# Routed attention and gated MLP on one core: f32 weights cast by GpSimd's DMAs instead of by the engines, in a new written order

## The chip, the cores and the metric

The kernel runs on one core of one Trainium2 chip. The metric is the device time of one execution, in microseconds (us). The engines are TensorE (PE in the profile, with its weight loads as PEld), VectorE (DVE), ScalarE (ACT), GpSimd (POOL) and SyncE (SP), which here only issues DMAs.

## The reference

Attention over 4 batches and 8 heads, 768 positions, head dimension 64. Each query and key is assigned to the nearest of 16 centroids of its head, and a query sees only keys of its own cluster. An MLP with a SiLU gate follows.

```python
q_assign = argmax(normalized(q) @ normalized(centroids).T)      # per head; the same for k
scores = where(q_assign[:, None] == k_assign[None, :], q @ k.T / 8, -1e9)
attn = softmax(scores) @ v                                      # [4, 8, 768, 64]
x = attn.transpose(0, 2, 1, 3).reshape(3072, 512)
h = x @ w_in                                                    # w_in [512, 2048], f32
out = (h * sigmoid(h)) @ w_out                                  # w_out [2048, 512], f32
```

## The kernel before, in words

All matmuls are in f16. Work is cut into steps: `step(engs, cost, fn, after, use, key)` notes a step with the engines that may run it (`"POOL/DVE/ACT"`), the steps it follows and the buffers it uses. Nothing is issued then. `Plan.emit` issues the steps in the sequence of a table, `ORDER`, with the engine that `CHOICE` names for each (the first one where it names none) and the buffer that `PLACES` gives. Negative entries of `ORDER` are filler matmuls on zeros: -1602 is 16 of them. So the order on each engine is written out by hand of a planner that is not part of the kernel; each engine works its own list strictly in that order, and so does each DMA queue. All loads but two, all stores and all DMA transposes are on SP's queue.

The steps, per pair of heads `p` and batch `b`:

- `load`: q, k and v in f32 to a buffer of the pool `raw` (8 buffers of 4 KB per partition, shared by q, k, v and, before, the weights).
- `part`: each row is split in two f16 halves, `hl` ("hi", a scaled copy, L295 to L297 or L291 by engine; "lo", the remainder, L441 on DVE). `hl` is transposed to `ab`: for the first pieces on PE (L466) with a copy back from PSUM, for all others by a DMA transpose of SP (L454). PE multiplies `ab` with the centroids (`stk`, `nstk`; L492, L493, L495), DVE takes the sum (L512), the peak (L523), marks the winner (`oh`, L536) and transposes the marks in 32 x 32 blocks (`ohT`, L550). Four "puts" write the marks into rows 64 to 79 of `ab`, so that the scores matmul itself carries the mask. A put runs on DVE (L295), POOL (L297) or ACT (L291).
- `attention`: scores on PE (L595), exp on ACT to `P` (L602), the product with v on PE (L612). `cast_values` makes `vt`, the f16 values, from `raw`.
- `normalize` (L631, L648) divides by the sums, to `xn`; `turn_x` transposes it to `xt`.
- `mlp`: up-projection on PE (L701) with `win_s`, tanh on ACT (`tn`, L712), the gate on DVE (`gq`, L715), down-projection on PE (L730) with `wout_s`, a copy to `ot` and a store (L745).
- `weight`: brings in one of the sixteen pieces of the MLP weights, 256 rows of 512 numbers as a 128 x 2 x 512 tile, 512 KB of f32. SP loads it to a `raw` buffer (L763), then POOL, DVE or ACT casts it to `win_s` or `wout_s` (L293 on POOL and DVE). `w_in_done` and `w_out_done` hold the step that the matmuls wait for.

The MLP of a batch follows that batch's attention, and in the order it is interleaved with the attention of later batches, so that PE has work while ACT does exp. Before its first real work PE runs the filler matmuls (`warm`, L853).

Of the kernel before, what the change touches and what calls it, by code (L numbers as in the profile page):

```python
# [17 lines left out]
BLOCKS = [[0, 2], [2, 6]]  # L18
UNITS = [[0, 4], [4, 6]]

ORDER = [
# [181 lines left out]
def kernel(  # L203
# [10 lines left out]
    nc = tc.nc  # L214
# [471 lines left out]
    def mlp(b, j0, j1, key):  # L686
# [36 lines left out]
        for t in range(j1 - j0):  # L723
# [26 lines left out]
            step("SP", ("store", 2048, 128), store, after=[x], use=[ot], key=-500)  # L750


    def weight(kind, n, key, after=()):
        x = buf("raw")

        def f(e):
# [128 lines left out]
```

## Time and profile before

| | us |
|---|---|
| three runs | 318.61, 319.30, 315.93 (median 318.61) |
| the profiled execution | 315.72, span 313.9 |
| PE, DVE, ACT, POOL busy | 297.7, 212.6, 221.0, 96.5 |
| first scores on PE, last matmul's end | 16.39, 310.34 |
| weight loads issued, first to last | 15.5 to 55.1 |
| weight casts on POOL (11) and DVE (5) | 12.6 and 4.0 |

The span runs from the first to the last instruction of the profiled execution, whose own time is 1.8 us longer. Busy time of PE includes matmuls that run slower than they could: their ends are modelled from the pipeline, so two matmuls that follow each other at any pace look like a busy engine. The table of 40 slices shows PE full from about 160 us on, with DVE and ACT dense before and thinner after it, and DMA engines full up to about 165 us.

### The profile page before, as it was taken

The numbers are of one execution on the slowest core, as the hardware profiler recorded it, in microseconds if no ns is written. First come the engines' busy times: TensorE is split into PE (matmuls) and PEld (weight loads), VectorE is DVE, ScalarE is ACT, GpSimd is POOL, SyncE is SP. The second block draws the span as 40 slices with busy tenths as digits, with TensorE's granted clock in tenths as the row PEclk, the third lists the DMA queues.
The fourth block names the chain that finished last, engine by engine and source line by source line (L and its number), as shares of the span: only waits on it lengthen the run. The fifth ranks groups of instructions, "written<-read, shape, count | busy, mean of one in ns | idle before, by whom it ended". The sixth has DMA issues, their size and how long they took to land.

```text
span 313.9 us, 7524 instructions
## 1 busy us (share of the span) xinstructions
PE 297.7 (95%) x2993; PEld 184.7 (59%) x2993; DVE 212.6 (68%) x476; ACT 221.0 (70%) x306; POOL 96.5 (31%) x175
## 2 busy tenths in 40 slices
PE   7799999997899999899899999999999999999995
PEld 5678675555546656657676465555665744555552
DVE  6978999987899898899799576232463532175230
ACT  3577989987799998699889869957787213264212
POOL 4875662544646364447226101300000000000000
PEclk9999999999999999999999999999999999999999
DMA  7989998969899999989992920000013021010023
GB/s 215 322 250 249 273 293 185 366 156 169 201 251 303 271 241 173 209 179 227 209 232 73 185 61 2 34 35 33 2 25 94 2 58 67 35 59 8 2 82 122
DMA packets 72852, 46.73 MB, mean 149 GB/s; under 512 B 52336, under 2 KB 65648, under 8 KB 72816
## 3 DMA queue, kind: packets, MB, share of 16 engines
q1 hardware_dynamic: 72528, 46.15, 59.2%
q8 instruction: 23, 0.38, 0.5%
q10 hardware_dynamic: 288, 0.10, 0.1%
q14 instruction: 13, 0.11, 0.1%
HBM read 27.30 MB, written 6.29 MB: 107 GB/s over the span
## 4 chain that ended last, share of the span: by engine, by line
PE 68%; DVE 11%; DMA 8%; POOL 5%; issue 3%; ACT 2%; SPq 1%; POOLq 0%; ACTq 0%; DVEq 0%
PE psum L730 23%; PE psum L701 22%; PE psum L595 14%; PE psum L612 7%; DMA ab<-hl 4%; DVE hl L441 2%; DMA raw<-in_k_dram 2%; POOL hl L297 2%; POOL ab L297 2%; PE psum L495 2%; DMA raw<-in_q_dram 2%; DVE gq L715 2%; DVE ab L295 1%; SPq L335 1%; DVE hl L295 1%
## 5 line engine op out<-in xcount | busy, mean ns | idle before, releaser
L602 ACT ACTIVATE P<-psum 128x1024 f16<-128x1024 f32 (+1 forms) x160 | 144.3, 942 | 24.5 <-PE psum L595 23.1
L715 DVE SCALAR_TENSOR_TENSOR gq<-tn,psum 128x512 f16<-128x512 f32 x96 | 63.2, 681 | 59.0 <-ACT tn L712 54.8
L701 PE MATMUL psum<-xt,win_s 128*128 128x256 f16 (+1 forms) x512 | 94.5, 325 | 1.3 <-DVE gq L715 1.0
L730 PE MATMUL psum<-wout_s,gq 128*128 128x512 f16 x384 | 90.9, 379 | 0.5 <-DVE wout_s L293 0.5
L595 PE MATMUL psum<-ab 80*128 80x256 f16 (+1 forms) x384 | 86.1, 339 | 3.1 <-POOL ab L297 2.2
L712 ACT ACTIVATE tn<-psum 128x512 f32<-128x512 f32 x96 | 56.0, 602 | 42.1 <-PE psum L701 39.7
L701 PEld LDWEIGHTS <-win_s 128*128 128x128 f16 x512 | 48.1, 97 | 33.1 <-issue 1.5
L297 POOL TENSOR_SCALAR ab<-ohT 16x384 f16<-16x384 f16 (+2 forms) x84 | 45.8, 546 | 62.0 <-DVE ohT L550 37.8
L730 PEld LDWEIGHTS <-gq 128*128 128x128 f16 x384 | 36.8, 97 | 41.4 <-issue 1.2
L612 PEld LDWEIGHTS <-P 128*128 128x128 f16 x1152 | 45.6, 99 | 13.4 <-issue 2.3
L612 PE MATMUL psum<-vt,P 128*128 128x65 f16 x1152 | 48.6, 195 | 1.9 <-POOL vt L293 1.2
L595 PEld LDWEIGHTS <-ab 80*128 80x128 f16 x384 | 34.6, 101 | 23.8 <-POOL ab L297 3.2
L441 DVE SCALAR_TENSOR_TENSOR hl<-raw,hl 128x384 f16<-128x384 f32 (+4 forms) x62 | 37.6, 622 | 8.3 <-POOL hl L297 7.9
L297 POOL TENSOR_SCALAR hl<-raw 128x384 f16<-128x384 f32 (+4 forms) x40 | 24.2, 609 | 25.6 <-DMA ab<-hl 9.2
L550 DVE STREAM_TRANSPOSE ohT<-oh 128x384 f16<-128x384 f16 (+2 forms) x33 | 18.5, 562 | 1.6 <-DVE oh L536 0.5
L648 DVE TENSOR_TENSOR xn<-psum,rz 128x384 f16<-128x384 f32 (+1 forms) x36 | 18.2, 509 | 0.8
L289 ACT COPY ot<-psum 128x512 f32<-128x512 f32 x14 | 8.1, 589 | 13.9 <-PE psum L730 13.7
L512 DVE TENSOR_REDUCE L<-psum 128x192 f32<-128x384 f32 (+1 forms) x28 | 14.9, 532 | 3.1 <-PE psum L495 2.7
L495 PEld LDWEIGHTS <-ab 128*128 128x128 f16 x320 | 11.7, 97 | 7.5 <-issue 2.4
L536 DVE TENSOR_TENSOR oh<-L,mx 128x96 f16<-128x96 f32 (+1 forms) x52 | 15.4, 313 | 0.6
L293 POOL CAST vt<-raw 128x384 f16<-128x384 f32 x23 | 12.7, 564 | 9.3 <-DMA raw<-in_v_dram 8.7
L295 DVE TENSOR_SCALAR ab<-ohT 16x384 f16<-16x384 f16 (+2 forms) x33 | 12.4, 375 | 0.9
(57 smaller groups left out, 146.4 us busy)
## 6 DMA issues: line engine op xcount, KB each, us to landing
raw<-in_v_dram SPq DMA_DIRECT2D x16, 384.0 KB, 4.8
out_dram<-ot SPq DMA_DIRECT2D x24, 256.0 KB, 2.3
raw<-in_k_dram SPq DMA_DIRECT2D x15, 384.0 KB, 5.5
raw<-in_q_dram SPq DMA_DIRECT2D x12, 384.0 KB, 4.6
raw<-in_moe_w_in_dram SPq DMA_DIRECT2D x8, 512.0 KB, 5.1
raw<-in_moe_w_out_dram SPq DMA_DIRECT2D x8, 512.0 KB, 5.6
raw<-in_q_dram SPq DMA_DIRECT2D x4, 256.0 KB, 5.2
ab<-hl SPq DMA_TRANSPOSE x28, 4.1
```

The source lines that it names most:

```text
L295: nc.vector.tensor_scalar(out=dst, in0=src, scalar1=scale, scalar2=None, op0=ALU.mult)
L297: nc.gpsimd.tensor_scalar(out=dst, in0=src, scalar1=scale, scalar2=1.0, op0=ALU.mult, op1=ALU.mult)
L441: (nc.vector if e == "DVE" else nc.gpsimd).scalar_tensor_tensor(out=dl, in0=src, scalar=scale, in1=dh, op0=ALU.mult, op1=ALU.subtract)
L550: nc.vector.transpose(t_(ohT)[:, 0:n, :].rearrange("p n c -> p (n c)"), t_(oh)[:, 0:n, :].rearrange("p n c -> p (n c)"))
L595: nc.tensor.matmul(o[:, w * (i - i0) : w * (i - i0 + 1)], t_(A)[0:80, kt[i], :], rhs, start=True, stop=True)
L602: nc.scalar.activation(out=t_(P)[:, 0:n], in_=o[:, 0:n], func=AF.Exp, bias=0.0, scale=-ESC)
L612: nc.tensor.matmul(bank(O)[:, D1 * (o0 + t) : D1 * (o0 + t + 1)], t_(P)[:, w * i + 128 * t : w * i + 128 * (t + 1)], t_(vb)[:, VW * j : VW ...
L648: nc.vector.tensor_tensor(out=x, in0=o, in1=z, op=ALU.mult)
L701: nc.tensor.matmul(bank(y)[:, n * (fb - f0) : n * (fb - f0 + 1)], win_s[:, r, ts(fb, 128)], t_(X)[:, r, 128 * j0 : 128 * j1], start=(r == ...
L712: nc.scalar.activation(out=t_(tn)[:, 0 : G * n], in_=bank(y)[:, 0 : G * n], func=AF.Tanh, bias=0.0, scale=1.0)
L715: nc.vector.scalar_tensor_tensor(out=t_(g)[:, f0 % 4 : f0 % 4 + G, 0:n], in0=t_(tn)[:, 0 : G * n].rearrange("p (g n) -> p g n", n=n), scal ...
L730: nc.tensor.matmul(bank(y), t_(gqs[quarter])[:, fc % 4, ts(t, 128)], wout_s[:, fc, :], start=(fc == 0), stop=(fc == NFB - 1),)
```

## The change

`SOFT = ['in', 'out']` names both weights. For these `weight` has one step instead of two: a DMA issued from GpSimd's queue that reads f32 from HBM and writes f16 straight to `win_s` or `wout_s`. No `raw` buffer and no cast belongs to it any more. The step waits for nothing. `ORDER`, `CHOICE` and `PLACES` are new throughout (1691 entries against 1704); the root of the centroids' norms also waits for the identity now. Line numbers of the kernel fall by one from the tables on (L295 is L294 now, L595 is L594), and rise by three after `weight`.

```diff
+SOFT = ['in', 'out']
 ORDER = [
-    4, 11, 21, 9, 1, 0, 18, 19, 6, 20, 22, 25, 23, 93, 94, 76, 12, 24, 78, 26, 13, 79, 77, 48, 91, 14, -1602, 80, 27,
...
-    s = step("POOL", ("c_root", 0), c_root, after=[s], key=-500)
+    s = step("POOL", ("c_root", 0), c_root, after=[s, s_ident], key=-500)
...
     def weight(kind, n, key, after=()):
+        r0, c0 = 2 * (n % 2), 512 * (n // 2)
+        if kind == "in":
+            src = moe_w_in.rearrange("(r p) f -> p r f", p=128)[:, r0 : r0 + 2, c0 : c0 + 512]
+            dst = win_s[:, r0 : r0 + 2, c0 : c0 + 512]
+        else:
+            src = moe_w_out[256 * n : 256 * n + 256, :].rearrange("(c p) d -> p c d", p=128)
+            dst = wout_s[:, 2 * n : 2 * n + 2, :]
+        done = w_in_done if kind == "in" else w_out_done
+        if kind in SOFT:
+
+            def h(e):
+                nc.gpsimd.dma_start(dst, src)
+
+            done.setdefault(n // 2, []).append(step("POOL", ("wload", 1024), h, after=after, key=key))
+            return
         x = buf("raw")
...
         s = step("SP", ("load", 2048, 256), f, after=after, use=[x], key=key)
         s = step("POOL/DVE/ACT", ("cast", 1024), g, after=[s], use=[x], key=key + 1)
-        (w_in_done if kind == "in" else w_out_done).setdefault(n // 2, []).append(s)
+        done.setdefault(n // 2, []).append(s)
```

By engine, the two orders differ so: fillers on PE 18 to 46; puts on DVE 33 to 54, on POOL 84 to 75, on ACT 15 to none but 3; splits of 128 x 384 on POOL 31 to 41, on DVE 12 to 7, on ACT 7 to 2; weight casts 16 to none; weight DMAs on POOL none to 16.

POOL's list after the root of the centroids' norms (`cy`), up to the first puts (`ab<-ohT`), which the first scores wait for. Before:

```order
L372 TENSOR_TENSOR cy<-cs,half 128x1
L297 TENSOR_SCALAR hl_85<-raw_78 128x6x64
L297 TENSOR_SCALAR hl_87<-raw_79 128x12x64
L297 TENSOR_SCALAR hl_87<-raw_81 128x4x64
L315 MEMSET vt_101 128x6
L297 TENSOR_SCALAR hl_86<-raw_82 128x12x64
```

And in the change:

```order
L371 TENSOR_TENSOR cy<-cs,half 128x1
L764 DMA wout_s<-in_moe_w_out_dram 128x2x512
L764 DMA win_s<-in_moe_w_in_dram 128x2x512 x2
L296 TENSOR_SCALAR hl_86<-raw_77 128x8x64
L314 MEMSET vt_99 128x6
L764 DMA win_s<-in_moe_w_in_dram 128x2x512
L296 TENSOR_SCALAR nstk<-stk 128x256
L314 MEMSET vt_93 128x6
L314 MEMSET vt_94 128x6
L314 MEMSET vt_101 128x6
L296 TENSOR_SCALAR hl_85<-raw_82 128x4x64
L296 TENSOR_SCALAR hl_87<-raw_83 128x12x64
```

Four weight DMAs and the negated centroids (`nstk`, which were DVE's) now stand there, and two more DMAs follow ahead of the first puts.

SP's list where the weights began. Before:

```order
L335 DMA raw_83<-in_v_dram 128x2x384
L454 DMA_TRANSPOSE ab_89<-hl_86 128x8x128
L763 DMA raw_82<-in_moe_w_in_dram 128x2x512
L335 DMA raw_81<-in_k_dram 128x2x384
L763 DMA raw_79<-in_moe_w_out_dram 128x2x512
L763 DMA raw_83<-in_moe_w_in_dram 128x2x512
```

And in the change, after the last of the first batch's v:

```order
L334 DMA raw_81<-in_v_dram 128x2x384
L453 DMA_TRANSPOSE ab_89<-hl_87 128x8x128
L334 DMA raw_83<-in_k_dram 128x2x384
L334 DMA raw_80<-in_q_dram 128x2x384
L453 DMA_TRANSPOSE ab_91<-hl_86 128x8x128
L334 DMA raw_78<-in_q_dram 128x2x384
```

Where weights were loaded to `raw`, k and q of the second batch are loaded now.

ACT's list from the 106th exp (`P`) on, with the tanh of the MLP (`tn`) between. Before:

```order
L602 ACTIVATE P_102<-psum 128x512
L602 ACTIVATE P_104<-psum 128x1024
L712 ACTIVATE tn_139<-psum 128x512
L602 ACTIVATE P_106<-psum 128x1024
L712 ACTIVATE tn_140<-psum 128x512
L602 ACTIVATE P_111<-psum 128x1024
L712 ACTIVATE tn_138<-psum 128x512
```

And in the change, from its 100th exp on:

```order
L601 ACTIVATE P_108<-psum 128x1024
L601 ACTIVATE P_114<-psum 128x1024
L288 COPY ot_142<-psum 128x512
L601 ACTIVATE P_104<-psum 128x1024
L601 ACTIVATE P_113<-psum 128x1024
L290 ACTIVATE hl_85<-raw_81 128x6x64
L601 ACTIVATE P_106<-psum 128x1024
```

From the 96th to the 138th exp no tanh stands in the new list: the up-projections that stood between now come later, behind the attention of later batches.

More of the change, by code (lines that the diff above doesn't have):

```diff
@@ L753, in weight @@
     def weight(kind, n, key, after=()):
+        r0, c0 = 2 * (n % 2), 512 * (n // 2)
[11 more added lines that the diff above has]
+            return
         x = buf("raw")
         def f(e):
-            dst = t_(x).rearrange("p (a c) -> p a c", a=2)
-            if kind == "in":
-                r0, c0 = 2 * (n % 2), 512 * (n // 2)
-                src = moe_w_in.rearrange("(r p) f -> p r f", p=128)[:, r0 : r0 + 2, c0 : c0 + 512]
-            else:
-                src = moe_w_out[256 * n : 256 * n + 256, :].rearrange("(c p) d -> p c d", p=128)
-            nc.sync.dma_start(dst, src)
-        def g(e):
-            src = t_(x).rearrange("p (a c) -> p a c", a=2)
-            if kind == "in":
-                r0, c0 = 2 * (n % 2), 512 * (n // 2)
-                copy(e, win_s[:, r0 : r0 + 2, c0 : c0 + 512], src)
-            else:
-                copy(e, wout_s[:, 2 * n : 2 * n + 2, :], src)
+            nc.sync.dma_start(t_(x).rearrange("p (a c) -> p a c", a=2), src)
+        def g(e):
+            copy(e, dst, t_(x).rearrange("p (a c) -> p a c", a=2))
         s = step("SP", ("load", 2048, 256), f, after=after, use=[x], key=key)
         s = step("POOL/DVE/ACT", ("cast", 1024), g, after=[s], use=[x], key=key + 1)
-        (w_in_done if kind == "in" else w_out_done).setdefault(n // 2, []).append(s)
+        done.setdefault(n // 2, []).append(s)
     def part0(p, segs, a0, key):
```

229 rows, old and new, of tables (CHOICE, ORDER, PLACES) are left out of this document.

## The prediction, written before the changed kernel ran

> **What bounds the kernel now.** I read the page's busy table first, then the chain of work that ended last, then a table of stages that I cut where the chain changes character (its columns: window and length, then busy time and count of PE, weight loads, DVE, ACT and POOL, the granted clock, the DMA share, GB/s).
>
> ```profile
> PE 297.7 (95%) x2993; PEld 184.7 (59%) x2993; DVE 212.6 (68%) x476; ACT 221.0 (70%) x306; POOL 96.5 (31%) x175
> ...
> PE 68%; DVE 11%; DMA 8%; POOL 5%; issue 3%; ACT 2%; SPq 1%; POOLq 0%; ACTq 0%; DVEq 0%
> ```
>
> TensorE (PE) is busy for 95% of the span, but on the chain for only 68%: part of its busy time is matmuls that run slowly. What its work costs at full rate comes from long pieces of the chain, in time order (start, length, what), with the counts of each shape:
>
> ```profile
> 155.79 1.02 PE psum L701 x4
> ...
> 243.81 2.00 PE psum L612 x66
> 245.81 0.87 PE psum L701 x8
> ...
> 249.80 8.63 PE psum L730 x40
> ...
> 310.41 0.59 ACT ot L289
> ```
>
> ```profile
> L730 PE MATMUL psum<-wout_s,gq 128*128 128x512 f16 x384 | 90.9, 379 | 0.5 <-DVE wout_s L293 0.5
> L701 PE MATMUL psum<-xt,win_s 128*128 128x512 f16 x256 | 63.2, 378 | 1.0 <-DVE gq L715 1.0
> L595 PE MATMUL psum<-ab 80*128 80x512 f16 x192 | 55.1, 379 | 0.7 <-POOL win_s L293 0.5 <-DVE L L512 0.2
> L612 PE MATMUL psum<-vt,P 128*128 128x65 f16 x1152 | 48.6, 195 | 1.9 <-POOL vt L293 1.2 <-DVE gq L715 0.6
> L701 PE MATMUL psum<-xt,win_s 128*128 128x256 f16 x256 | 33.7, 272 | 0.3 <-DVE win_s L293 0.2
> L595 PE MATMUL psum<-ab 80*128 80x256 f16 x192 | 32.9, 299 | 2.4 <-POOL ab L297 2.2 <-DVE ab L295 0.2
> ```
>
> A 512-wide matmul costs 8.63/40 = 0.216 us, a 256-wide one 0.87/8 = 0.108, a value matmul (L612) 2.00/66 = 0.030. So 832 x 0.216 + 448 x 0.108 + 1152 x 0.030 = 263 us; the 448 logit matmuls and 94 transposes add an estimated 22 (they are as narrow as L612, or a 128-wide piece). **PE's own work is about 285 us.** The span is 313.9. From 155.8 to 310.4 the chain is PE almost alone, 3.5 us follow; so before 155.8 PE does about 285 - 154.6 = 130 us of work and **loses about 26 us there**. That loss is all that the change can win. Where it lies:
>
> ```profile
> 0.00:16.40 16.40, 11.60 (x131) 9.20 (x131) 13.27 (x39) 8.00 (x9) 10.23 (x31) 1.00 0.97 258
> 16.40:30.80 14.40, 14.40 (x181) 11.63 (x182) 12.00 (x26) 10.92 (x15) 9.29 (x15) 1.00 0.94 259
> 30.80:86.50 55.70, 50.65 (x628) 32.61 (x625) 49.73 (x118) 48.72 (x62) 29.61 (x44) 1.00 0.94 235
> 86.50:126.60 40.10, 40.01 (x462) 24.28 (x461) 36.86 (x86) 37.77 (x54) 19.97 (x37) 1.00 1.11 249
> 126.60:155.80 29.20, 26.54 (x348) 18.36 (x345) 26.17 (x66) 25.21 (x36) 14.63 (x26) 1.00 0.95 204
> 155.80:310.40 154.60, 154.53 (x1256) 88.58 (x1255) 74.61 (x146) 89.79 (x135) 12.81 (x25) 1.00 0.22 61
> ```
>
> The first scores run at 16.4, when PE has done under 7 us of real work: some 10 lost. PE then stands still for 5.1 us up to 86.5 and 2.7 up to 155.8. The remaining 8 are matmuls at a slower pace, mostly between 16.4 and 30.8, where PE counts as busy throughout. In the same stages VectorE (DVE) and ScalarE (ACT) are 83 to 94% busy: after 16 us three engines share the bound.
>
> **The change part by part.** It takes away sixteen f32 loads of SP and sixteen casts (11 on GpSimd (POOL), 5 on DVE). Sixteen transfers enter POOL's list, and the order is new throughout. By count from the two orders: ACT loses 15 copies of one-hot marks ("puts"), and 22 instructions in all; DVE gains 21 puts (33 to 54) and loses its 5 weight casts; POOL gains 10 splits of 384 and loses 9 puts.
>
> *Term 1, first scores.* They are released at 16.4 by POOL's puts.
>
> ```profile
> L297 POOL TENSOR_SCALAR ab<-ohT x84: 399/507/938, 13.8 to 198.7; 16x384 f16<-16x384 f16 x63, 16x256 f16<-16x256 f16 x15, 16x512 f16<-16x512 f16 x6
> L293 POOL CAST win_s<-raw x6: 1042/1110/1591, 29.2 to 42.6; 128x1024 f16<-128x1024 f32 x6
> L763 SPq DMA_DIRECT2D raw<-in_moe_w_in_dram x8: 367/368/627, 15.5 to 37.2; - x8
> ```
>
> Now six weight transfers stand ahead of these puts, and with them four splits, the negated centroids and three puts: 5.0 us by their durations. The chain reaches that place about 6 us in, so the first scores come at 11 + 6d, with d the time a transfer holds POOL. No row of before shows d. The nearest are the issue of the same 128x2x512 shape on SP (0.37) and POOL's own pass over that shape (1.04). With 0.37 it is 13.2, and DVE's list, which carries eleven split instructions before the first peak (seven today), decides at about 15.4. I take 1.0, since the same POOL cores have 256 rows to describe: 17.0, **+0.6**. Bounds: -1.0, and +6.6 at d = 2.
>
> *Term 2, slow matmuls.* Early 256-wide matmuls take twice the 0.108 above:
>
> ```profile
> 16.39 2.91 PE psum L595 x12
> 19.30 1.71 PE psum L466 x16
> ...
> 21.84 2.15 PE psum L595 x10
> ...
> 25.49 1.31 PE psum L595 x6
> ```
>
> These 28 take 6.4 us where 3.0 would do, the 16 transposes up to 0.9 more: 4.3, though the granted clock reads 1.00. The new list puts 31 filler matmuls first (16 before) and 15 more between the setup's PE steps (2 before). If that holds the full pace, up to 4.3 are won; ACT, 76% busy there, then takes over. I take **-2.5**; bounds 0 and -4.3.
>
> [...]
>
> *Term 3, loads.* Weights no longer hold raw buffers, and SP issues batch 1's q, k and v where weights stood. Today's longest hole follows from late transfers:
>
> ```profile
> 70.62 5.47 DMA ab<-hl
> ...
> 77.33 4.89 DMA raw<-in_q_dram
> ```
>
> Most of the 5.1 us that PE stands still before 86.5 lies there: **-3**, bounds 0 and -5. That the weights arrive late instead I cost at nothing: the first up-projection has 22 us of PE work ahead of it, its transfers are issued at 11 us or less of PE work; the last one at 33, and the first down-projection comes at 40.
>
> *Term 4, the two engines that exclude each other.*
>
> ```profile
> L295 DVE TENSOR_SCALAR ab<-ohT x33: 217/255/1133, 21.0 to 191.9; 16x384 f16<-16x384 f16 x21, 16x256 f16<-16x256 f16 x7, 16x512 f16<-16x512 f16 x5
> L441 DVE SCALAR_TENSOR_TENSOR hl<-raw,hl x62: 293/558/1267, 2.9 to 173.3; 128x384 f16<-128x384 f32 x50, 128x512 f16<-128x512 f32 x4, 128x768 f16<-128x768 f32 x3, 128x256 f16<-128x256 f32 x3
> L295 DVE TENSOR_SCALAR hl<-raw x15: 227/618/1265, 2.7 to 170.3; 128x384 f16<-128x384 f32 x12, 128x512 f16<-128x512 f32 x2, 128x128 f16<-128x128 f32 x1
> L536 DVE TENSOR_TENSOR oh<-L,mx x52: 241/257/622, 30.5 to 192.2; 128x96 f16<-128x96 f32 x48, 128x128 f16<-128x128 f32 x4
> ```
>
> Instructions of one shape range from 241 to 622 ns and from 217 to 1133; the long ones overlap POOL work. Over these groups the time above the free duration is some 10 us (estimated from these spreads). POOL's eleven 1 us casts go; an order that pairs POOL with PSUM reads of DVE removes more. Half of it, at the half of the places where PE waits: **-2**, bounds 0 and -5.
>
> *Term 5, attention ahead of the MLP.* 348 MLP matmuls stand before the 288th scores matmul today, 196 in the new list, so some 26 us less PE work covers the same work of DVE and ACT. Counted with free durations, DVE's list before that point is 147 us against 152 of PE today, and 131 against 126 in the new one. In its fullest stage DVE was busy 36.86 of 40.10, and lost some 4% of that to term 4: 0.88 free work per us. So DVE needs 131/0.88 + 4 (first data) = 153 us: a loss of 27. With both nearly perfect, 0.93, it is 145: a loss of 19. Terms 1 to 4 alone give 26 + 0.6 - 2.5 - 3 - 2 = 19. I take 22 in all, between the sum and the floor: **+3** for this term; bounds 0 and +8.
>
> ACT's 22 instructions fewer I cost at nothing: ACT is 2% of the chain, and what it gives up goes to DVE, where term 5 has it.
>
> **Sum.** 285 + 22 + 3.5 = 310 us of span, 4 less than today. The profiled execution took 315.72 for 313.9 of span, so 312 for it; the median of the runs, 318.61, is 0.9% above the profiled one: **314.8 us**. A measurement of this kernel tells about 1% from no change (its three runs lie 1.1% apart).
>
> **Rivals.**
> *Better:* fillers keep PE fast and the exclusion is nearly gone; loss 17, 309.7 us. For it: term 2's doubled times and the spreads of term 4. Against: it needs DVE 93% effective for 145 us on end, more than any stage above.
> *No change:* terms 1 and 5 eat the rest; loss 25.5, 318 us. For it: DVE and ACT are above 90% where PE runs without a hole.
> *Slower, DVE is the bound:* DVE keeps 0.86, its average of today's four stages from 16 to 156 (125 of 139 busy, less the 4%), so 131/0.86 + 4 = 156, a loss of 30, 323 us. It decides below 0.875. For it: 21 more puts. Against: 5 casts fewer.
> *Slower, the transfers hold POOL and DVE:* with d = 2 or more the puts come 6.6 us late, and each transfer that falls on a DVE write lengthens it by up to the 1.27 - 0.56 of the longest split, 16 x 0.7 = 11, a third of it felt: loss 26 + 6.6 - 2.5 - 3 + 4 = 31, 324 us. It decides from d of about 1.6. Against: after 31 us POOL is half idle, and ten of the sixteen stand there.
>
> [...]
>
> **How the numbers follow.** Forecast (loss 20 to 24) 0.31; better 0.17; no change 0.21; DVE bound 0.15; transfers hold POOL 0.16. Faster by over 1% (below 315.4): 0.17 + 0.26 of the forecast's 0.31 = 0.43. Within 1%: 0.21 + 0.05 = 0.26, less 0.01 for its slow edge: 0.25. Slower: 0.32. The range, 305.5 to 326, leaves about a tenth on each side; the forecast's own is 313 to 317.
>
> **What would show it.** Right: first scores near 17; 256-wide matmuls at 0.108 from the first scores on; no hole after a q load near 75 us; DVE above 92% busy to 140 us with PE's idle time put down to DVE; about 22 us lost by 155 us. Wrong: a transfer that holds POOL for over 1.6 us, first scores past 19, PE waiting on `win_s`, or holes before scores in the stretch without tanh.

## The result, and the profile after

The changed kernel takes **333.16 us** (median of 4 runs, 330.77 to 337.05) against 318.35 for the kernel before on the same chip: a ratio of **1.047** (1.042 to 1.052). A run that lies over 1.5% above the fastest of its kernel (here 337.05) counts as slow and is left out of the ratios. The forecast was 314.8, in a range of 305.5 to 326. The profiled execution took 333.93, with a span of 332.1. The first lines below are the page's busy time, chain, queues and transfers of the changed kernel, to be held against those of before:

```profile
PE 302.1 (91%) x3021; PEld 185.5 (56%) x3021; DVE 214.9 (65%) x490; ACT 212.1 (64%) x287; POOL 95.1 (29%) x180
...
q1 hardware_dynamic: 68176, 37.76, 51.1%
q0 software_dynamic: 4352, 4.20, 8.1%
...
PE 60%; DMA 17%; DVE 15%; issue 4%; ACT 2%; SPq 1%; POOL 1%; DVEq 0%; POOLq 0%; ACTq 0%
PE psum L700 23%; PE psum L729 21%; DMA ab<-hl 15%; PE psum L594 9%; PE psum L611 5%; DVE hl L440 4%; DMA raw<-in_v_dram 2%; DVE xn L647 2%; DVE ab L294 2%; DVE ohT L549 2%; ACT P L601 1%; DVE oh L535 1%; PE psum L494 1%; DVE gq L714 1%; DVE L L511 1%
...
wout_s<-in_moe_w_out_dram POOLq DMA_DIRECT2D x8, 256.0 KB, 7.2
win_s<-in_moe_w_in_dram POOLq DMA_DIRECT2D x8, 256.0 KB, 9.5
...
ab<-hl SPq DMA_TRANSPOSE x28, 5.0
```

VectorE (DVE) and ScalarE (ACT) do what the two orders promised (ACT 212 us instead of 221). PE has its old work and 28 more fillers, but is busy for 91% instead of 95%, and DMA has gone from 8% of the chain to 17%; 15% is one thing, `ab<-hl`, the transposes that SP's queue makes of the split keys and queries. What PE waited for (us in total, times, longest), after and, in the second fence, before:

```profile
PE psum L494 <- DMA ab<-hl: 13.3, 6, 5.7
PE psum L594 <- DVE ab L294: 2.2, 3, 1.1
```

```profile
PE psum L595 <- POOL ab L297: 2.2, 1, 2.2
PE psum L495 <- DMA ab<-hl: 1.5, 2, 0.8
```

The wait for these transposes grew from 1.5 us to 13.3. Where it lies shows in the table of stages (columns as in the prediction):

```profile
0.00:17.40 17.40, 13.29 (x167) 10.34 (x167) 12.16 (x37) 9.70 (x12) 11.40 (x30) 1.00 0.95 249
17.40:30.80 13.40, 10.43 (x154) 8.38 (x155) 11.38 (x30) 9.36 (x13) 7.23 (x14) 0.75 1.24 206
30.80:40.00 9.20, 8.64 (x128) 6.19 (x126) 8.90 (x25) 8.28 (x12) 7.25 (x13) 1.00 1.18 208
40.00:72.00 32.00, 22.33 (x247) 14.28 (x244) 19.95 (x49) 17.52 (x21) 13.30 (x24) 0.84 1.06 186
72.00:126.60 54.60, 51.16 (x662) 32.95 (x661) 51.28 (x123) 48.38 (x63) 28.12 (x49) 0.97 0.99 197
126.60:180.00 53.40, 47.85 (x627) 30.54 (x624) 49.08 (x124) 45.50 (x60) 26.80 (x50) 1.00 0.87 194
180.00:328.00 148.00, 147.94 (x1053) 82.85 (x1052) 62.15 (x108) 72.75 (x113) 0.96 (x2) 1.00 0.13 41
```

From 40 to 72 us PE is busy for 22.3 of 32, and at a granted clock of 0.84. In the chain, one piece (two transposes, the second issued while the first was under way) fills most of that stage, and the matmuls behind it show both costs, the hole and the slow pace (start, length, what; then PE's rows with the idle time before them):

```profile
41.03 20.70 DMA ab<-hl x2
```

```profile
55.45 0.60 PE L594 MATMUL psum<-ab 80*128 80x512 f16 x2
61.78 0.34 PE L494 MATMUL psum<-nstk,ab 128*128 128x32 f16 x6 [5.72 <-DMA ab<-hl]
...
62.92 3.62 PE L700 MATMUL psum<-xt,win_s 128*128 128x256 f16 x16
```

PE stands 5.7 us before the logits at 61.78, and the row behind them has 3.6 us for sixteen 256-wide matmuls, which cost 16 x 0.108 = 1.7 at full pace. The rows of SP's queue say why the transposes were late; the number behind the start is how long SP was held by that one instruction, not how long its data took. After, then before:

```profile
36.08 1.23 SPq L453 DMA_TRANSPOSE ab<-hl  x1
...
47.24 4.92 SPq L453 DMA_TRANSPOSE ab<-hl  x1
52.21 0.58 SPq L334 DMA_DIRECT2D raw<-in_k_dram  x1
52.89 8.38 SPq L453 DMA_TRANSPOSE ab<-hl  x1
```

```profile
43.34 1.23 SPq L454 DMA_TRANSPOSE ab<-hl  x1
44.62 0.57 SPq L763 DMA_DIRECT2D raw<-in_moe_w_out_dram  x1
48.73 3.41 SPq L454 DMA_TRANSPOSE ab<-hl  x2
```

In this stage a transpose holds SP for 1.2 to 2 us before (the last row is two of them), and for 1.2 after at 36, where no weights are on their way; the one at 52.89 holds it for 8.4. From issue to landing, the transposes of this stage took 4.1 us before; after, those issued at 41.03, 47.24 and 52.89 took 8.8, 14.5 and 11.2. The logits at 61.78 waited for the second of these, which landed at 61.74; the third stood behind it in the queue. While SP was held by the third, the DMA queues moved this, on SP's queue mostly the second one's data (queue, packets, MB, share of 16 engines; window 52.9 to 61.3):

```profile
q0 software_dynamic: 1124, 1.07, 75.8%
q1 hardware_dynamic: 1499, 0.47, 46.8%
```

Per packet that is 0.758 x 16 x 8.4 / 1124 = 0.091 us on GpSimd's queue (q0: weights, 1 KB each) and 0.042 on SP's (q1: 256 B and a few longer ones). The packets come in like numbers while both queues have work: 962 and 974 from 53 to 59 us (from 60 to 61, where GpSimd's queue has 11 left, SP's moves 187). So **the two queues move as many packets of one as of the other, as in turns**, and a transpose's short packets come only at the pace of the weights' long ones: 974 in 6 us, or 162 a microsecond. In the kernel before, the two transposes at 48.73 had SP's queue to themselves, and it moved this while they held SP (window 48.7 to 52.2):

```profile
q1 hardware_dynamic: 1644, 0.43, 74.4%
```

That is 470 packets a microsecond. The weights stood in the same queue there (the load at 44.62), and a transpose near them held SP for no more than 2 us. The like numbers agree with turns of like size; how many records of the trace make one turn they do not show. The prediction did not weigh this.

To see where the time goes, I follow what PE has lost at each point: the time at which a step starts, less PE's own work before it (priced as in the prediction). Columns: own work done, then the loss in us.

```
own work   before   after   old order,    new order,    old order,
 done                       no weights    no weights    casting transfers
   16        15.0    15.4      14.4          17.3          15.3
   24        15.9    16.3      16.3          17.1          16.2
   32        17.3    22.4      17.7          17.4          16.3
   40        17.7    31.1      18.0          20.7          25.2
   64        22.2    32.9      22.4          22.4          28.0
  104        22.5    38.3      22.7          26.7          28.3
  136        25.6    43.4      26.1          32.7          30.4
  all        25.5    43.7      26.0          32.7          30.4
```

In these profiled executions the change loses 18 us more than before (the medians lie 14.8 apart): 13.0 between 24 and 40, it wins 2.7 between 40 and 64, and it loses 7.1 more between 64 and 136. The last three columns are from experiments that follow.

### The profile page after: what moved, and what is told of

Its sections match the earlier page's. It is cut to its first block, busy times and chain, and to the rows that moved or that the text cites. A ratio compares the mean times of both kernels' runs of the same rounds, so it can differ in the third digit from the quotient of the medians.

```text
span 332.1 us, 7536 instructions
## 1 busy us (share of the span) xinstructions
PE 302.1 (91%) x3021; PEld 185.5 (56%) x3021; DVE 214.9 (65%) x490; ACT 212.1 (64%) x287; POOL 95.1 (29%) x180
## 3 DMA queue, kind: packets, MB, share of 16 engines
q1 hardware_dynamic: 68176, 37.76, 51.1%
q0 software_dynamic: 4352, 4.20, 8.1%
## 4 chain that ended last, share of the span: by engine, by line
PE 60%; DMA 17%; DVE 15%; issue 4%; ACT 2%; SPq 1%; POOL 1%; DVEq 0%; POOLq 0%; ACTq 0%
PE psum L700 23%; PE psum L729 21%; DMA ab<-hl 15%; PE psum L594 9%; PE psum L611 5%; DVE hl L440 4%; DMA raw<-in_v_dram 2%; DVE xn L647 2%; DVE ab L294 2%; DVE ohT L549 2%; ACT P L601 1%; DVE oh L535 1%; PE psum L494 1%; DVE gq L714 1%; DVE L L511 1%
## 5 line engine op out<-in xcount | busy, mean ns | idle before, releaser
L700 PE MATMUL psum<-xt,win_s 128*128 128x256 f16 (+1 forms) x512 | 96.4, 334 | 1.2 <-DVE gq L714 1.1
L594 PE MATMUL psum<-ab 80*128 80x256 f16 (+1 forms) x384 | 87.3, 338 | 5.0 <-DVE ab L294 2.2
L700 PEld LDWEIGHTS <-win_s 128*128 128x128 f16 x512 | 50.0, 100 | 36.4 <-issue 2.8
L296 POOL TENSOR_SCALAR ab<-ohT 16x384 f16<-16x384 f16 (+2 forms) x75 | 40.6, 542 | 40.8 <-DVE ohT L549 20.5
L594 PEld LDWEIGHTS <-ab 80*128 80x128 f16 x384 | 33.5, 100 | 22.6 <-issue 3.2
L440 DVE SCALAR_TENSOR_TENSOR hl<-raw,hl 128x384 f16<-128x384 f32 (+4 forms) x62 | 40.2, 658 | 6.1 <-POOL hl L296 5.8
L296 POOL TENSOR_SCALAR hl<-raw 128x384 f16<-128x384 f32 (+3 forms) x48 | 27.5, 579 | 31.6 <-DMA ab<-hl 12.0
L292 DVE COPY ot<-psum 128x512 f32<-128x512 f32 x11 | 7.6, 691 | 34.5 <-PE psum L729 31.2
L294 DVE TENSOR_SCALAR ab<-ohT 16x384 f16<-16x384 f16 (+2 forms) x54 | 19.9, 368 | 1.4
L494 PE MATMUL psum<-nstk,ab 128*128 128x32 f16 x144 | 7.5, 178 | 12.3 <-DMA ab<-hl 10.9
```

The source lines that it names most:

```text
L294: nc.vector.tensor_scalar(out=dst, in0=src, scalar1=scale, scalar2=None, op0=ALU.mult)
L296: nc.gpsimd.tensor_scalar(out=dst, in0=src, scalar1=scale, scalar2=1.0, op0=ALU.mult, op1=ALU.mult)
L440: (nc.vector if e == "DVE" else nc.gpsimd).scalar_tensor_tensor(out=dl, in0=src, scalar=scale, in1=dh, op0=ALU.mult, op1=ALU.subtract)
L594: nc.tensor.matmul(o[:, w * (i - i0) : w * (i - i0 + 1)], t_(A)[0:80, kt[i], :], rhs, start=True, stop=True)
L700: nc.tensor.matmul(bank(y)[:, n * (fb - f0) : n * (fb - f0 + 1)], win_s[:, r, ts(fb, 128)], t_(X)[:, r, 128 * j0 : 128 * j1], start=(r == ...
```

## The experiments

Theory Q, formed from the rows above (in the first expectations its rougher form is called A): the weights, moved to a queue of their own, take turns with the transposes on the same DMA engines and make them late. Its rivals: the new written order is at fault (B); the cast inside the transfer costs (C); the bytes cost wherever they are. Ratios are to the kernel before on the same chip, with 95% intervals.

### The order and the transfers apart

**New order, no weights.** `nc.gpsimd.dma_start(dst, src)` becomes `nc.gpsimd.memset(dst, 0.01)`.

> The changed kernel's order, with each of the sixteen casting transfers replaced by a memset of the same weight tile on GpSimd: no weight leaves the DRAM, so what the MLP computes leaves the weights out. Theory A (the casting transfers slow SP's queue, so its transposes land late): the time falls by 10 us or more from the changed kernel's 333, to 316-323, and the transposes' rows on SP's queue shrink from 3-8 us back towards 1.2. Theory B (the new order is at fault: transposes stand behind loads, attention stands ahead of the MLP): it stays at 328-333, with holes before the logits near 42, 48 and 56-62 us.

Measured: 322.8 us, 1.017 (1.014 to 1.021), the slow end of theory A (Q's first form). SP's transposes:

```profile
41.59 1.42 SPq L453 DMA_TRANSPOSE ab<-hl  x1
45.34 1.44 SPq L453 DMA_TRANSPOSE ab<-hl  x1
47.78 1.43 SPq L453 DMA_TRANSPOSE ab<-hl  x1
```

```profile
PE psum L494 <- DMA ab<-hl: 2.6, 2, 2.0
```

The same three held SP for 3.0, 4.9 and 8.4 us with the transfers running, and landed 8.8, 14.5 and 11.2 us after issue; here it is 4.3, 3.8 and 4.7. So the transfers cost 10.4 us here (9.5 by the ratios); what stays is the order's own, 6.0 us against the next run, which theory A had not asked for. A memset holds GpSimd for 0.95 us, a transfer for 0.76, so GpSimd had no less to do.

**Old order, no weights.** The loads issue nothing and take no `raw` buffer; each cast becomes a memset on its engine.

> The kernel before with the sixteen weight loads left out and each cast replaced by a memset of the same tile on the same engine: what the weights cost the old order. Theory A: weights share one queue with everything else there and cost little, 312-317 against 318. Theory B: 315-319. If it falls below 308, the weights' bytes themselves bound the first 70 us of either kernel, and the kind of transfer matters less.

Measured: 316.8 us, 0.998 (0.995 to 1.002). **The weights' transfers cost the old order nothing that can be measured.** There was nothing for a better transfer to win. (The casts' time on the engines is not in this: a memset takes about as long, 0.97 to 1.02 us on GpSimd where a cast took 1.11 to 1.20.) The page's line for SP's queue, without weights and in the second fence with them (before), tells what they take of the engines:

```profile
q1 hardware_dynamic: 68176, 37.76, 50.8%
```

```profile
q1 hardware_dynamic: 72528, 46.15, 59.2%
```

(0.592 x 313.9 - 0.508 x 314.5) x 16 / (72528 - 68176) = 0.096 us a packet, for 4352 packets. The casting transfers are 4352 packets too, and 0.081 x 332.1 x 16 / 4352 = 0.099 us each: half the bytes are written, but **the cast makes the transfer no cheaper for the engines**, as far as the packets' times show it (packets of two queues overlap: in the window above their shares are 75.8% and 46.8%, more than 100% together).

**Old order, casting transfers.**

```
 def f(e):   # the load step
-    nc.sync.dma_start(dst, src)
+    nc.gpsimd.dma_start(weight_tile, src)
 def g(e):   # the cast step
-    copy(e, ...)
+    pass
```

> The kernel before in its own order; the sixteen weight loads become casting transfers from GpSimd's queue at the loads' places in the order, and the casts are gone. The half of the change that is the transfers, without the new order. Theory A: 324-332, with holes before the logits while the transfers run. Theory B: 314-319, no slower than the kernel before, since sixteen casts and SP's waits for raw buffers go.

Measured: 320.7 us, 1.010 (1.007 to 1.013): between the two. The direction is A's, the size is not. PE's wait for transposes went from 2.0 (no weights) to 9.3 us, and the loss table shows 7 us more lost between 24 and 40, but the old order gives some of it back. One of its transposes:

```profile
46.52 6.02 SPq L454 DMA_TRANSPOSE ab<-hl  x1
```

The queues' packets come in like numbers here too, 980 and 965 from 46 to 53 us. So the order costs 6.0 us alone, the transfers 3.9 alone, without any casts on the engines (both against the old order without weights), and together 16.4 (15.5 by the ratios): neither theory alone, and more than their sum.

### What it is in the transfers

**Old order, plain f32 loads from GpSimd's queue**, cast on chip as before: `nc.sync.dma_start(dst, src)` becomes `nc.gpsimd.dma_start(dst, src)` for the weights.

> The kernel before with its sixteen weight loads issued from GpSimd's queue, still plain f32 into the raw buffers and cast on chip: a second queue, but no casting transfer. Theory Q (the packets of two queues alternate one for one, so a transpose of 1536 packets of 256 B runs at the pace of the weights' long packets, whatever these carry): 320-327, with transposes on SP's queue of 3 us and more where the weights run. Theory C (it is the cast in the transfer that costs): 316-319, transposes as before.

Measured: 326.6 us, 1.023 (1.016 to 1.030), with two transposes of 5.5 and 6.6 us:

```profile
52.88 5.50 SPq L454 DMA_TRANSPOSE ab<-hl  x1
```

```profile
58.43 6.60 SPq L454 DMA_TRANSPOSE ab<-hl  x1
```

PE's wait for transposes is 9.7 us, as with the casting transfers (9.3). No cast in the transfer, and the same harm: the second queue does it, not the cast. (GpSimd also waits for raw buffers in this kernel, which the 326.6 holds as well.) But the packets do not come one for one in this run: from 57 to 64 us they are 236 of some 3.5 KB against 1091 of SP's queue. So Q's rule of like numbers holds for the casting transfers, and by what rule these plain ones stretch a transpose stays open.

**Half as long packets in the new order.**

```
-nc.gpsimd.dma_start(dst, src)        # moe_w_out
+for c in range(0, 512, 256):
+    nc.gpsimd.dma_start(dst[:, :, c : c + 256], src[:, :, c : c + 256])
```

> The changed kernel with each of the eight transfers of moe_w_out as two of half the columns: the same bytes, packets of 512 B instead of 1024, twice as many. Theory Q: a transpose's packet waits for a weight packet of half the length, so the 8.4 us transpose near 53 takes 5 to 6 and the hole of 5.9 us before the logits shrinks to 2-4: 327-331, the eight more 0.75 us on GpSimd included. Theory bytes (the engines are full, and what counts is the bytes ahead): no change, 332-335.

Measured: 330.2 us, 1.039 (1.036 to 1.042), against 1.047. PE stands 3.0 us before the same logits instead of 5.7, as forecast; the transpose at that place holds SP for 7.3 us instead of 8.4, less of a gain than the 5 to 6 forecast, and later ones stretch (5.2 and 3.7): weight packets still run beside them, 710 against 822 of SP's queue from 60 to 63 us. Right in direction; the packet's length is not the whole of it.

**New order, only `moe_w_in` transferred** (`moe_w_out` a memset).

> The changed kernel with the eight transfers of moe_w_out replaced by memsets on GpSimd; those of moe_w_in stay. Theory Q puts nearly all of the transfers' 10 us on the moe_w_out ones, which run beside the transposes of 41 to 61 us: 322-326. If the moe_w_in ones (7 to 35 us) cost as much, 327-330.

Measured: 322.6 us, 1.014 (1.010 to 1.017), the same as without any weights. The transfers' 10 us belong to the eight of `moe_w_out`. Those of `moe_w_in` still stretch the transpose at 11 us to 6.9 (1.3 without weights), and PE waits 6.1 us for transposes in all (2.6 without weights), but the end does not feel it.

**Transfers early in the old order**: each `moe_w_out` transfer right behind the `moe_w_in` one of its number.

> The old order with casting transfers, each moe_w_out transfer issued right behind the moe_w_in one of its number, so all sixteen by about 35 us instead of 56. The three transposes that took 14.3 us from 42 on then find fewer weight packets. Theory Q (the harm lies in the overlap in time, not in the number of transfers): those three take 4-8 us, 316-319.5. If the transfers cost through GpSimd or in any place alike: 320-322, as with the transfers at the loads' places (320.7).

(The 14.3 us in that text is a row of three transposes with the gaps between them; singly they took 1.2, 6.0 and 3.8.) Measured: 319.4 us, 1.005 (1.001 to 1.009), the three at 1.2, 1.4 and 2.9 us, PE's wait for transposes 1.6 us instead of 9.3. So in the old order the wait can be put out of the way. In time that is little: 1.005 against 1.010, intervals that overlap, and the profiled execution was the fastest of the ten (316.1).

**Transfers early in the new order**: seven `moe_w_out` entries moved up the table, nothing else.

```
-... 122, ... 648, ... 137, ... 665, ... 663, ... 653, ... 178, ...
+... 122, 45, ... 648, 47, ... 137, 48, ... 665, 46, ... 663, 51, ... 653, 49, ... 178, 50, ...
```

> The changed kernel with seven of the eight moe_w_out transfers moved up in the order, spread over 22 to 36 us of GpSimd's list instead of 40 to 52; nothing else moves. Theory Q: the transposes after 41 us, which took 3.0, 4.9 and 8.4 us, come down to 1.2-2.5 each and those at 32 and 36 stretch from 1.2 to 3-6, where less hangs on them; 323-328. If a transfer costs the same wherever it stands: 331-335.

Measured: 334.3 us, 1.053 (1.046 to 1.059). A miss: it is no better than the change.

```profile
31.85 4.42 SPq L453 DMA_TRANSPOSE ab<-hl  x1
...
39.47 6.88 SPq L453 DMA_TRANSPOSE ab<-hl  x1
...
49.33 3.41 SPq L453 DMA_TRANSPOSE ab<-hl  x1
```

The stretched transposes moved with the transfers, as Q says, but "less hangs on them" was wrong: PE then waits 3.4 us from 32 and 3.5 from 44 (10.8 in all). The chain of this run has a transpose from 22 to 35.7 us and then a load of keys, on SP's queue like the transposes:

```profile
46.40 7.43 DMA raw<-in_k_dram
```

So in the new order the moved transfers meet other urgent work of SP's queue, and not transposes alone.

### PE's pace

**Fillers in the holes** of the changed kernel (12, 14 and 40 ahead of the late logits).

> The changed kernel with 12, 14 and 40 filler matmuls on zeros ahead of the three late groups of logits (holes at 40.4-42.1, 47.6-49.9 and 55.5-61.8 us). If the halved matmul pace after these holes is a clock that dropped because TensorE stood idle, some 18 steps at double time between 50 and 68 us come back: 326-329. If the pace has another cause, or the fillers themselves come into the way: 332-336.

Measured: 330.3 us, 1.029 (1.023 to 1.035). The four runs fall apart: 325.8 and 327.4, on which the ratio rests, are within the first forecast (some 6 us by the ratio), while 333.3 and 333.8 are no better than the change. So that part of the loss behind a hole is PE's own pace is likely, and its size uncertain.

**Fillers in the kernel before**: 20 at the start instead of 16, and 12 ahead of the first scores (`-2002` for `-1602`, and `-1201` before entry 625).

> The kernel before with 20 filler matmuls at its start (16 before) and 12 more just ahead of the first scores, in the 2.4 us in which TensorE stands still there. Term 2 alone, in the old order. If TensorE's pace is a matter of having been busy, the 28 slow 256-wide matmuls up to 28 us come at 0.108: 313.5-316 against 317. If being busy is not enough (it is busy without a hole from 16.4 to 28 today and stays slow), 316.5-318.

Measured: 315.0 us, 0.991 (0.988 to 0.994). The same kernel again, with more runs, and with the 12 alone:

> The kernel before with the fillers at the start and ahead of the first scores, once more with more rounds: 0.991 was measured over 4 runs, and 0.995 without the four fillers at the start. If the gain is one of the code: 0.988-0.995. If it was the spread between programs: 0.996-1.002.

> The kernel before with only the 12 fillers ahead of the first scores, its 16 at the start unchanged. If the gain of the run with both (0.991) comes from keeping TensorE busy just ahead of the first scores: 0.989 to 0.995. If the four more at the start made it, or it was the spread between builds: 0.997 to 1.003.

Measured: 315.7 us, **0.993** (0.990 to 0.996), and 0.995 (0.991 to 0.999) with the 12 alone. That last ratio rests on seven of twelve runs; the other five took 319.5 to 320.7, and the median of all twelve, 317.6, is no lower than before (317.3), so a gain by the 12 alone is not shown. The group of early 256-wide matmuls, before and in the repeated run (16.4 to 30 us; busy, mean ns of one):

```profile
L595 PE MATMUL psum<-ab 80*128 80x256 f16 x36 | 8.7, 414 | 2.2 <-POOL ab L297 2.2
```

```profile
L595 PE MATMUL psum<-ab 80*128 80x256 f16 x42 | 5.9, 273 | 3.5 <-POOL ab L297 2.3 <-DVE ab L295 1.2
```

414 ns become 273 (331 in the profiled execution of the first run of this kernel). How slow the clock was shows in the old order without weights, where the same group also has a mean of 414 ns (stage from 16.2 to 29.9, columns as above; the 0.50 is the granted clock):

```profile
16.20:29.90 13.70, 13.62 (x171) 10.90 (x171) 11.36 (x24) 10.29 (x14) 9.11 (x15) 0.50 0.48 122
```

In the repeated run it is 1.00 from 16.4 to 30.8. This version beats both kernels, the one before by 0.7%; what the four fillers at the start add and what the 12 do is open.

**Both at once**, early casting transfers and fillers in the old order.

> The early casting transfers in the old order, with the fillers at the start and ahead of the first scores as well: a candidate for a version that beats both. If the two effects add up: 313.5-316.5. If the transfers' own POOL time ahead of 35 us takes the fillers' gain: 317-320.

Measured: 319.1 us, 1.003 (0.999 to 1.007). They don't add up: with transfers on GpSimd's queue the fillers' gain is gone.

### The order's own six microseconds

**26 puts from VectorE to GpSimd**, in the new order without weights (26 entries of `CHOICE` left out).

> The changed kernel's order without weight traffic (memsets on GpSimd, as in the first run, 1.017 of before), and the last 26 puts that VectorE does there (0.34 us each, 9 us) go to GpSimd instead (0.55 each). What the new order itself costs: if VectorE is the bound from 80 us on, because attention stands ahead of the MLP, two to four us come back, 1.005 to 1.011 of before (318.5-320.5). If VectorE is not the bound, or GpSimd's puts come later than VectorE's did, no change or slower, 1.015 to 1.025.

Measured: 324.0 us, 1.021 (1.015 to 1.027): no gain. PE now waited 5.0 us for puts on GpSimd, so this run doesn't tell whether VectorE's list was the bound.

**Half of the last 32 residual splits**, in both orders without weights (`src, dh, dl` cut to `[:, 0 : NJ // 2]` for batches 2 and 3).

> The changed kernel's order without weight traffic, and each of the last 32 residual splits that VectorE does (those of batches 2 and 3, 128x384, 0.56 us each) made half as wide, so half of the residuals is left out: some 8 us less for VectorE from about 95 us on, nothing later than before. Theory D (with attention ahead of the MLP, VectorE's list sets the pace from 60 to 170 us): 4 to 7 us come back, 1.017 of before falls to 0.995-1.005 (316-319). Rival (the order's 6 us are transfers and cold matmuls, VectorE only looks busy): 1.011 or more.

> The same cut in the old order without weight traffic (0.998 of before without the cut). Theory D: VectorE has slack there from 87 us on, 0 to 2.5 us come back, 0.990-0.998. Rival: the cut brings as much here as in the new order.

Measured: 319.5 us, 1.004 (1.001 to 1.008), and 314.5 us, 0.988 (0.985 to 0.992). The first is inside theory D's range, but the second is the rival's: the cut brought 1.3% in the new order and 1.0% in the old one, which cannot be told apart. The new order's busy times over the stage in question (64 to 137 us of PE's own work), without and with the cut:

```profile
87.00:170.00 83.00, 76.10 (x986) 48.14 (x985) 77.27 (x189) 71.37 (x93) 42.05 (x75) 0.98 0.90 195
```

```profile
85.00:168.00 83.00, 77.23 (x1000) 49.61 (x996) 71.96 (x190) 71.93 (x95) 38.80 (x76) 0.96 0.92 197
```

VectorE had 5.3 us less to do in 83 us, and PE gained 1.1. By the loss, the new order still loses 9.5 us between 64 and 136 of own work (10.3 without the cut). **Theory D is not shown**: VectorE stands in the new order's chain throughout, but making it faster does not free PE in proportion. What the order's 6 us wait for stays open.

## Right and wrong, step by step

**Term 1 (first scores), right in size, in part by luck.** First scores at 17.44 us, forecast near 17. The transfer's hold on GpSimd was forecast at 1.0 us, a choice of the author's between two rows; that it goes by a transfer's rows was not shown (all sixteen have 256). The row of the eight says 0.76 (minimum, median, maximum in ns; first and last start):

```profile
L764 POOL DMA_DIRECT2D win_s<-in_moe_w_in_dram x8: 716/759/771, 8.1 to 45.6; - x8
```

The longest of all sixteen is 0.93 us. By the prediction's 11 + 6d that gives 15.6; the puts ahead of the first scores came later because GpSimd waited for VectorE's marks (start, length, count; idle time before and what ended it):

```profile
16.05 1.34 POOL L296 TENSOR_SCALAR ab<-ohT 16x256 f16<-16x256 f16 x3 [0.64 <-DVE ohT L549]
```

So VectorE's list decided, which the prediction had at about 15.4, and not the transfers' hold. The last rival, that transfers hold GpSimd and VectorE, came near the time (324) by a way that didn't happen: it decides from 1.6 us. The lengthening of VectorE's writes that it adds was not shown either: in the changed kernel's trace four 128x384 splits with over 450 ns of a transfer's hold beside them took 544 to 553 ns; a fifth, with a split of GpSimd's beside it as well, took 855.

**Term 2 (slow matmuls, -2.5), wrong in this kernel.** At 16 us of own work the loss is 15.4, against 15.0 before. The full pace was there at first and went again: the granted clock is 0.75 from 17.4 to 30.8, which is 1.00 up to 23.4 and 0.50 from 23.6 to 30.3, and it is 0.50 once more from 61.2 to 67.8, behind the longest hole. In the old order, where no such holes follow, fillers bring some 2 us (0.991 and 0.993), so -2.5 was about the size of the gain there. The clock records of the changed kernel's trace, but for the one at the end, last 3.41 us or multiples of it (3.41 from 50.8, 6.83 from 61.1). What brings the full pace no run shows: in the kernel before, PE is by the profile busy without a hole for 11 us from 16.4 and slow throughout (414 ns against 273 with the fillers). (The granted clock of 1.00 that the prediction quotes for that stretch is no sign against a halved clock: the trace of before has no clock record ahead of 30.7 us, and in the old order without weights, just as slow there, it reads 0.50.)

**Term 3 (loads), the step that failed.** The forecast -3 did come where it was forecast: the hole near 75 is gone, and between 40 and 64 the change loses 1.8 where before lost 4.5. But it came with the new order; freed buffers alone do not bring it: the old order without weights, in which no weight takes a buffer, still loses 4.4 there (18.0 to 22.4). And the sentence "that the weights arrive late instead I cost at nothing" asked the wrong question. No weight was late (PE never waited on `win_s`). The weights made **others** late: the transposes, whose `hl`-to-`ab` chain feeds the logits. Sixteen transfers were priced by what they hold of GpSimd and at nothing on the DMA engines, though the quoted stages had the DMA share at 0.94 to 0.97 up to 86 us. On those full engines the transfers, in a queue of their own, moved as many packets as SP's queue (962 against 974). The term should have held some +10 for that: PE waits 13.3 us for transposes, and 2.6 in the same order without weights, which is 10.4 us faster.

**Term 4 and term 5** were forecast at -2 and +3. What term 4 is named for stands in the trace of before: VectorE's 128x384 splits took 541 to 559 ns where no GpSimd work ran beside them, and up to 1267 where it did; its gates, which read PSUM, took 640 to 690 without and 646 to 690 with it. Between 64 and 136 of own work the change loses 7.1 us more than before, and 6.9 more without any weights. That is near term 5's upper bound (+8) and leaves nothing of term 4 to see. Whether term 5's step, that VectorE sets the pace there, holds stays open: VectorE is indeed busy for 94% from 72 to 126.6 (51.28 of 54.60), but that this is what PE waits for is not shown.

**The sum** was 3.9 us less loss than before, and is 18.2 more in the profiled executions. By the stretches of the table, the 22 us between are: up to 24 of own work +0.4 instead of terms 1 and 2 together, -1.9; from 24 to 40 +13.0 instead of nothing; from 40 to 64 -2.7 where term 3 had -3; behind that +7.1 instead of terms 4 and 5 together, +1. The second of these is the miss: with it right, the forecast would have stood near 328. No rival had it, so the range missed the time.

**The signs.** Right: first scores, the hole at 75. In part: VectorE's share, 94% from 72 to 126.6 but 62% from 40 to 72, and PE's idle time is put down to the transposes, not to VectorE. Wrong: matmuls at 0.108 from the first scores on, and a loss of 22. "Holes before scores" was close to the sign that came: holes before the logits. One reading of the prediction was off: in the stages after 16 us ScalarE and VectorE are 76 to 94% busy, not 83 to 94% (ScalarE 10.92 of 14.40 in the first).

## What to carry to other kernels

Before a transfer is moved to another queue, ask which short transfers it will then run beside: on the full DMA engines of this kernel a queue of its own was also a share of the packets (962 against 974), and bulk weights that waited their turn in the same queue as small urgent transposes did less harm than on a queue of their own. Leave the suspected cost out first (here the weights, in the old order): a run that gains nothing by it shows that no better way of paying that cost can gain either, in that order. An order written out by hand has its slack in certain places, and a change of the traffic and a change of the order are to be measured apart, since here they cost 3.9 and 6.0 us alone and 16.4 together.

## What the runs showed of the hardware

- Two DMA queues with work, one with casting transfers, moved packets in like numbers: 962 against 974 in 6 us, and 980 against 965 in 7 us in the old order. A transpose that landed 4.1 us after its issue in the same stage before landed after 8.8 to 14.5. With plain loads of 3.5 KB packets the numbers were not alike (236 against 1091).
- A casting transfer costs the DMA engines as much as the plain one: 0.099 us a packet against 0.096, at the same 4352 packets. It lands in 7.2 to 9.5 us (5.1 and 5.6 for the plain loads before, 5.2 and 5.9 for plain loads from GpSimd's queue).
- A transfer of 256 rows holds GpSimd for 0.72 to 0.93 us.
- TensorE can be busy by the profile for 11 us on end at half its pace, with a granted clock of 0.50 where the trace records it; fillers ahead of that stretch bring the mean of its 256-wide matmuls from 414 ns to 328, 331 and 273 in three profiled executions.
